# Attention followed by an ELU layer on one core: value matmuls ahead of the first step, an earlier weight block, and later slots for batch 2's transposes

## The chip, the cores and the metric

The kernel runs on one core of a Trainium2 chip. The metric is the device time of one execution in microseconds. Before: 322.39 us, the median of three executions (322.37 to 322.59). Each execution also reports its span (device time less some 1.7 us of start and end) and the mean clock granted to TensorE, where 1.0 is full speed. All executions in this study are of the state called fast; the last sections show that this name covers two groups with different clocks.

## The reference, cut to what matters

```python
scores = scale * q @ k.T + alibi_bias       # 8 batches, 8 heads, 576 positions, 64 per head
mask = (rel >= 0) & (rel < 128)             # each position sees itself and the 127 before it
attn = softmax(where(mask, scores, -1e9)) @ v
x = attn.transpose(0, 2, 1, 3).reshape(4608, 512)
h = x @ w_in                                # 512 -> 2048
out = where(h > 0, h, exp(min(h, 0)) - 1) @ w_out    # 2048 -> 512
```

## The kernel before

It is one hand-made schedule. Its slots are numbered, and a slot holds one group of hidden products (`x @ w_in`, L250), pieces of attention, and one group of output products (L269). Instructions reach each engine in the order in which they are emitted. A batch's q and k come in by DMA as `st`, and VectorE turns them to `QT` and `KT` (L139) for all batches from the third on (batch 2, counted from 0); the first two are turned by TensorE (L131). PSUM is the memory that TensorE writes its results to, in banks. The parts that matter here, with cuts marked:

```python
def turn_qk(b, w, h2, dh, ...):             # L139: VectorE transpose of a quarter of q or k
    V.transpose(o, st[b][...])              # needs all four loads of that q or k
def first_weigh(b, u, half):                # L183: the "product", exponentials times the bias table
    V.tensor_tensor(out=e, in0=e, in1=TAB[...], op=ALU.mult)
def values(b, i, part, bank=av):            # L215 on TensorE, then VectorE:
    ...                                     # L221 reciprocal, L222 normalization to xn
def turn(b, i, copy, bank):                 # L234 transpose of xn on TensorE, L235 copy to xT
    ...
def hidden(t, c0, w, f0, nf, p):            # L250, then L255 exponential on ScalarE,
    ...                                     # L256 clamp on GpSimd
def elu(...):                               # L263 on VectorE: g, which frees the PSUM bank p
    ...
# one slot: early tasks, hidden products, g of the slot before, tasks, output products, late tasks
```

"Freed product" below means the first L183 of batch 1 (slot 19): the values of slot 20 wait for it.

The softmax here doesn't subtract the row's maximum and nothing guards it: scores larger than these inputs give would overflow.

## Time and profile before

| What | Before |
|---|---|
| Median device time | 322.39 us |
| Span of the profiled execution | 320.7 us |
| TensorE busy | 312.4 us, 97% |
| TensorE's waits after the start | 3.1 us in all |
| Mean clock of the profiled execution | 1.00 |

TensorE's busy share leaves nothing to overlap: a wait that goes away shortens the kernel unless a later wait takes the gain back, and any other engine's busy time matters only where TensorE waits for it. So the list of TensorE's waits (who waits, for whom, us in all, how many, the longest) and the timelines around each one are the views to read. They are shown in the prediction. A line of a timeline has start, duration, engine, source line, operation, output and inputs, shape, count; a bracket gives the idle time before it and what ended it.

### The profile page before, as it was taken

How to read it: one execution, taken by the hardware profiler on the slowest of the kernel's cores; microseconds unless marked ns; L12 is line 12 of the kernel's file. 1: busy time of each engine (PE TensorE's matmuls, PEld its weight loads, DVE VectorE, ACT ScalarE, POOL GpSimd, SP SyncE). 2: the span in 40 equal slices, each digit the busy share in tenths (PEclk: the TensorE clock that was granted, in tenths of full speed). 3: DMA queues.
4: the chain of work that ended last, by engine and by line, in shares of the span. 5: the costliest groups of instructions: out<-in, count | busy, mean ns of one | idle time of the engine just before them, and what ended most of it. 6: DMA issues, size and time to landing. Idle time of an engine off the chain costs nothing.

```text
span 320.7 us, 9636 instructions
## 1 busy us (share of the span) xinstructions
PE 312.4 (97%) x4072; PEld 222.3 (69%) x4072; DVE 218.6 (68%) x446; ACT 183.9 (57%) x327; POOL 166.2 (52%) x254
## 2 busy tenths in 40 slices
PE   7999998999999999999999999999999999999996
PEld 7678873787777777777666666676677666766653
DVE  5457656888877877777877787778777566653330
ACT  6777456775655465556666666646654655543431
POOL 8467768284656546563756365655633333333320
PEclk9999999999999999999999999999999999999999
DMA  8999999977799939795979878994911111110012
GB/s 102 201 193 207 192 166 147 113 76 100 84 92 125 127 52 118 97 120 88 98 96 124 114 84 90 125 131 68 108 51 51 44 50 51 51 57 35 33 59 74
DMA packets 94043, 32.02 MB, mean 100 GB/s; under 512 B 81840, under 2 KB 89520, under 8 KB 94000
## 3 DMA queue, kind: packets, MB, share of 16 engines
q0 software_dynamic: 73600, 18.36, 62.6%
q1 hardware_dynamic: 20400, 13.05, 15.5%
q8 instruction: 32, 0.52, 0.7%
q14 instruction: 11, 0.09, 0.1%
HBM read 36.70 MB, written 9.44 MB: 144 GB/s over the span
## 4 chain that ended last, share of the span: by engine, by line
PE 91%; DVE 2%; POOL 2%; ACT 2%; DMA 1%; issue 0%; DVEq 0%; POOLq 0%; ACTq 0%
PE hp L250 38%; PE op L269 19%; PE av L269 16%; PE sp L215 4%; PE spa L192 4%; PE op L289 2%; POOL e L256 1%; DMA st<-in_k_dram 1%; PE sp L269 1%; PE spa L167 1%; PE av L283 1%; DVE xn L222 1%; ACT e L255 1%; DVE g L263 1%; PE sp L250 1%; POOL VP L109 1%
## 5 line engine op out<-in xcount | busy, mean ns | idle before, releaser
L256 POOL TENSOR_SCALAR e<-e 128x512 f32<-128x512 f32 x144 | 90.1, 626 | 141.2 <-ACT e L255 140.6
L250 PEld LDWEIGHTS <-wi 128*128 128x128 f16 x1856 | 124.5, 98 | 35.3 <-issue 5.2
L250 PE MATMUL hp<-xT,wi 128*128 128x128 f16 (+2 forms) x1760 | 146.0, 233 | 0.6 <-DVE g L263 0.6
L263 DVE SCALAR_TENSOR_TENSOR g<-e,hp 128x512 f16<-128x512 f32 x139 | 95.0, 683 | 56.1 <-POOL e L256 54.6
L255 ACT ACTIVATE e<-hp 128x512 f32<-128x512 f32 x139 | 83.3, 599 | 86.5 <-PE hp L250 83.4
L269 PE MATMUL op<-wo,g 128*128 128x512 f16 x304 | 77.5, 379 | 0.0
L269 PEld LDWEIGHTS <-g 128*128 128x128 f16 x560 | 50.1, 98 | 36.7 <-issue 1.1
L269 PE MATMUL av<-wo,g 128*128 128x512 f16 x240 | 61.4, 379 | 0.0
L203 DVE TENSOR_TENSOR EX<-EX,TAB 128x1024 f16<-128x1024 f16 x48 | 33.1, 690 | 15.4 <-ACT EX L198 15.3
L109 POOL DMA_DIRECT2D VP<-in_v_dram x40 | 35.0, 878 | 1.8 <-DMA wi<-in_moe_w_in_dram 1.3
L198 ACT ACTIVATE EX<-spa 128x512 f16<-128x512 f32 x48 | 26.1, 594 | 16.4 <-PE spa L192 16.4
L222 DVE TENSOR_TENSOR xn<-sp,rden 128x256 f16<-128x256 f32 (+1 forms) x60 | 25.4, 424 | 2.1
L198 ACT ACTIVATE EX<-sp 128x512 f16<-128x512 f32 x48 | 26.1, 600 | 0.0
L215 PEld LDWEIGHTS <-EX 128*128 128x128 f16 x576 | 22.3, 97 | 3.6 <-DVE EX L183 2.9
L215 PE MATMUL sp<-VP,EX 128*128 128x65 f16 x428 | 18.9, 193 | 1.3 <-DVE EX L183 1.3
L139 DVE STREAM_TRANSPOSE KT<-st 128x576 f16<-128x576 f16 x24 | 18.1, 801 | 2.0 <-DMA st<-in_k_dram 2.0
L139 DVE STREAM_TRANSPOSE QT<-st 128x576 f16<-128x576 f16 x24 | 18.3, 802 | 0.0
L276 ACT COPY ob<-op 128x512 f32<-128x512 f32 x19 | 11.1, 586 | 9.5 <-PE op L269 9.2
L103 POOL DMA_DIRECT2D st<-in_k_dram x24 | 16.5, 688 | 0.1
L103 POOL DMA_DIRECT2D st<-in_q_dram x24 | 16.3, 682 | 0.0
L192 PEld LDWEIGHTS <-KT 32*128 32x128 f16 x480 | 8.9, 93 | 10.4 <-issue 10.2
L192 PE MATMUL spa<-QT,KT 32*128 32x256 f16 (+2 forms) x240 | 14.7, 248 | 0.0
(88 smaller groups left out, 189.2 us busy)
## 6 DMA issues: line engine op xcount, KB each, us to landing
out_dram<-ob SPq DMA_DIRECT2D x35, 256.0 KB, 2.4
VP<-in_v_dram POOLq DMA_DIRECT2D x32, 128.0 KB, 4.4
st<-in_k_dram POOLq DMA_DIRECT2D x24, 144.0 KB, 3.5
st<-in_q_dram POOLq DMA_DIRECT2D x24, 144.0 KB, 4.0
wi<-in_moe_w_in_dram POOLq DMA_DIRECT2D x4, 512.0 KB, 12.0
wo<-in_moe_w_out_dram POOLq DMA_DIRECT2D x4, 512.0 KB, 11.7
s<-in_q_dram POOLq DMA_DIRECT2D x2, 384.0 KB, 9.3
VP<-in_v_dram POOLq DMA_DIRECT2D x8, 64.0 KB, 4.1
```

What stands on the lines that cost most here:

```text
L103: nc.gpsimd.dma_start(st[b][32 * g:32 * g + 32, w, :, :, :, :].rearrange("p h n j d -> p (h n) (j d)"), (q, k)[w][b, 2 * g:2 * g + 2, :, : ...
L109: nc.gpsimd.dma_start(VP[b % 2][0:p, n, :, 0:D], v[b, :, 128 * n:128 * n + p, :].rearrange("h p d -> p h d"))
L139: V.transpose(o, st[b][:, w, h2, n0:n1, :, 32 * dh:32 * dh + 32])
L192: nc.tensor.matmul(sp[g][:, 256 * h2 + o:256 * h2 + o + n], kt_[b % 2][r, k0:k0 + 128], QT[b % 2][r, h2, dh, q0:q0 + n], start=dh == 0, st ...
L198: nc.scalar.activation(unit(b, u)[:, g, :, :], sp[g].rearrange("p (h c) -> p h c", h=2), AF.Exp, scale=0.125)
L203: V.tensor_tensor(out=e, in0=e, in1=TAB[:, int(u == 3), 2 * gp:2 * gp + 2, :, :], op=ALU.mult)
L215: nc.tensor.matmul(a[:, x, h2, :], ex_[u][:, c:c + 128], VP[b % 2][:, n, 2 * g + h2, 0:D + 1], start=j == 0, stop=j == len(parts) - 1)
L250: nc.tensor.matmul(p[:, l * w + u0:l * w + u1], w_in_sb[:, c, fc * 128:(fc + 1) * 128], xT[:, c, x0:x0 + u1 - u0], start=(c == 0), stop=(c ...
L255: nc.scalar.activation(e[:, 0:n], p[:, 0:n], AF.Exp)
L256: nc.gpsimd.tensor_scalar(out=e[:, 0:n], in0=e[:, 0:n], scalar1=1.0, scalar2=0.0, op0=ALU.min, op1=ALU.max)
L263: V.scalar_tensor_tensor(out=gs[t][:, f0:f0 + nf, c0:c0 + w], in0=sh(es.pop((t, c0, f0))), scalar=1.0, in1=sh(hps.pop((t, c0, f0))), op0=A ...
L269: nc.tensor.matmul(o, gs[t][:, fc, ts * 128:(ts + 1) * 128], w_out_sb[:, fc, :], start=(fc == 0), stop=(fc == NFC - 1))
```

## The change

Its intent: let the first half of the second tile's values run before the first hidden step, so that their normalization is done earlier; bring the third quarter of `w_in` sooner; and keep batch 2's transposes out of the way of the product, with their loads sooner.

```diff
         load_first(0, 0, 1)
+        load_wi(2)
         load_v(0, 2)
-        load_wi(2)
         load_wi(3)
@@
         for half in range(2):
             first_expo(0, 1, half, half, 0, 128)
+        values(0, 1, 0)
@@
-        at(0, values, 0, 1, 0)
         at(0, values, 0, 1, 1, op)
@@
-        for n, s in enumerate((6, 7, 11, 12, 14)):
+        for n, s in enumerate((6, 7, 11, 12, 13)):
             at(s, load_v, 1, n)
@@
-        TURN = 18, 18, 22, 23, 24, 25, 26, 28
+        TURN = 19, 22, 23, 24, 24, 25, 27, 29
@@
-                at(a - 8 + n if a else 15 + (n + 1) // 2, load_qk, b, int(n < 4), n % 4)
+                at(a - 8 + n if a else 14 + n // 2, load_qk, b, int(n < 4), n % 4)
             for n in range(5):
-                at(a + 3 + n if a else 19 + n, load_v, b, n)
+                at(a + 3 + n if a else 18 + n // 2, load_v, b, n)
```

I call the three parts part 1 (values), part 2 (`w_in`) and part 3 (slots and loads of batch 2).

## The prediction

> **What bounds the kernel now.** I read the head of the page first, then who TensorE waited for, then the timeline around each wait that is left.
>
> ```profile
> PE 312.4 (97%) x4072; PEld 222.3 (69%) x4072; DVE 218.6 (68%) x446; ACT 183.9 (57%) x327; POOL 166.2 (52%) x254
> ...
> PEclk9999999999999999999999999999999999999999
> ```
>
> TensorE is busy for 312.4 of 320.7 us, with the full clock granted in every slice. From 76 us to the final output matmuls it has no gap, so a change before 76 us is worth just what it takes off the moment at which that stretch begins. The change removes no work. Its ceiling is thus TensorE's waits before 76 us, which the table of TensorE's waits lists in full:
>
> ```profile
> PE op L289 <- DVE ident L312: 1.6, 1, 1.6
> PE sp L215 <- DVE EX L183: 1.3, 1, 1.3
> PE op L234 <- DVE xn L222: 1.0, 1, 1.0
> PE hp L250 <- DVE g L263: 0.6, 2, 0.3
> PE spa L161 <- ACT EX L172: 0.2, 1, 0.2
> ```
>
> The columns are us in all, how often, and the longest. The first, 1.6 us, is the start of the kernel and isn't touched. The rest is 3.1 us, or 1.0% of 322.39: no outcome near 2% faster is in reach. The change aims at the second line (batch 2's transposes) and the third (the second tile's values). How the second arises shows in the timelines of TensorE and VectorE:
>
> ```profile
> 50.65 1.04 PE L269 MATMUL sp<-wo,g 128*128 128x512 f16 x4
> 53.02 0.30 PE L215 MATMUL sp<-VP,EX 128*128 128x65 f16 x4 [1.34 <-DVE EX L183]
> ...
> 48.66 1.02 ACT L172 ACTIVATE EX<-spa 128x1024 f16<-128x1024 f32 x1 [0.94 <-PE spa L167]
> ...
> 50.93 1.49 DVE L139 STREAM_TRANSPOSE KT<-st 128x576 f16<-128x576 f16 x2 [2.00 <-DMA st<-in_k_dram]
> 52.32 0.65 DVE L183 TENSOR_TENSOR EX<-EX,TAB 128x1024 f16<-128x1024 f16 x1
> ```
>
> The exponentials that the product (L183) weighs are ready at 48.66 + 1.02 = 49.68 us. VectorE starts it at 52.32, since two transposes of batch 2 stand before it in its queue and wait for the fourth load of k, issued at 47.67 and landed 3.1 us later. TensorE's values wait for the product.
>
> The third wait:
>
> ```profile
> 14.24 1.07 PE L250 MATMUL hp<-xT,wi 128*128 128x128 f16 x16
> 15.14 0.41 PE L215 MATMUL av<-VP,EX 128*128 128x65 f16 x8
> 15.39 0.40 PE L215 MATMUL op<-VP,EX 128*128 128x65 f16 x8
> 16.83 0.38 PE L234 MATMUL op<-ident,xn 128*128 128x128 f16 x4 [1.04 <-DVE xn L222]
> 17.05 1.95 PE L250 MATMUL hp<-xT,wi 128*128 128x128 f16 x32
> ...
> 16.03 0.61 POOL L256 TENSOR_SCALAR e<-e 128x512 f32<-128x512 f32 x1 [3.30 <-ACT e L255]
> 16.70 0.68 DVE L263 SCALAR_TENSOR_TENSOR g<-e,hp 128x512 f16<-128x512 f32 x1
> 17.29 0.42 DVE L235 COPY xT<-op 128x512 f16<-128x512 f16 x1
> ```
>
> The second tile's transpose (L234) waits for the two normalizations that follow the two halves of its values.
>
> **What the Trainium skill says.** "TensorE: Matmul & The Clock Gate", in the table that opens it (engine queue depth): VectorE's queue is strictly first in, first out. The trace agrees: a product ready at 49.68 starts at 52.32. The same page, Part 2, back-to-back issue gap: N/2.4 + 2.5 ns, so 216 ns at N = 512. The L269 groups agree (58.31 to the next group at 59.17: 4 in 0.86 us). So the values at 53.02 could have issued at 50.65 + 0.88 = 51.53, and the stall is worth 1.49 us, more than the 1.34 shown, which counts from a modelled end. "GPSIMD Engine Reference", section 1: GpSimd shares its SBUF interface with VectorE. The trace agrees: L256 takes 0.61 us mostly, but 1.00 at 70.56, where a product runs on VectorE.
>
> **Part 1, half of the second tile's values ahead of the first step.** TensorE now does 8 value matmuls at 14.24 (0.25 us), then 16 of the first step from 14.49, then the other 8 from 15.39 as before. The operands are there: the half's exponentials end at 13.86, its v landed at 9.3. The first half's reciprocal and normalization move from 15.59 to about 14.7, out of the way. The second half's start when its matmuls end, 15.82; 0.18 + 0.42 us and hand-overs give 16.44 instead of 16.77. The transpose issues at 16.50 instead of 16.83: 0.33 gained. But the first step's matmuls end 0.25 later, and so do its exponential (15.59 to 16.19), GpSimd's clamp (16.28 to 16.89) and VectorE's g (from 16.95 instead of 16.70). The order of VectorE's instructions is unchanged here, and g stands ahead of the copy of the transposed tile to xT. The copy starts 0.59 after g, at 17.54, and ends at 17.96. The second 16 of the 32 matmuls at 17.05 need that copy. Before they issued at 17.05 + 0.89 = 17.94; now TensorE is ready at 17.62 and held to about 18.01. Part 1: 0.07 us lost, in effect nothing.
>
> **Part 2, w_in's third quarter ahead of v.** From the issues and their times to landing: that quarter landed at 8.28 + 13.1 = 21.4 us and its first use is the step at 23.32, without a wait. It will land near 20.5; the v block it passes lands near 21.4, against a use at 25.56. The first copies' order in the queue is otherwise unchanged. Worth 0.
>
> **Part 3, batch 2.** Its loads go out one to three slots sooner, the fourth k load at about 44.0 instead of 47.67. The data in flight before it (the last v of batch 1, three k loads) landed by 49.35; 144 KB more at the some 180 GB/s of this stretch is 0.8 us, so it lands between 48 and 50.2. VectorE does the product at 49.73 to 50.40, and one transpose from 50.33 to 51.15. The values issue at 51.53 instead of 53.02: 1.49 gained. VectorE is free again before their reciprocal is due at 51.87, so the next product runs 52.43 to 53.11 and the next values at 53.16 instead of 54.66: the gain holds. From there to 60.9 TensorE and VectorE alternate by the same chain as before, all 1.49 earlier.
>
> What comes back: the displaced transpose lands in slot 24 (slots are the kernel's own schedule steps), where VectorE had little room. In times of the before trace: transposes at 61.29 and 62.03, g at 62.75 (was 62.00), product at 63.33 (was 62.58), another transpose at 63.92, and then g of slot 25 from 64.66 to 65.35 (was 64.31 to 65.00). The hidden product of slot 27, at 65.14, reuses that g's PSUM bank: it starts at 65.40, 0.26 lost. The later moves (27 and 29 for 26 and 28) fall behind products that TensorE then waits less for. The wait of 0.26 at 72.33 stays: it follows matmul, exponential, a clamp of 1.0 and g. GpSimd issues two loads between clamps in slots 14 to 17; 2 x 0.67 + 0.61 = 1.95 us against a slot of 1.75 delays the clamps of 15 and 16 by 0.1 to 0.2 us, which their buffers, a ring of three, take up.
>
> **Sum.** 322.39 + 0.07 - 0 - 1.49 + 0.26 = 321.23 us.
>
> **Rivals.** (A) Part 1 pays in full: were the copy not behind g, 0.33 would be kept, and the time 320.8. For it: the 1.04 us wait is real. Against: the copy's place in VectorE's queue. (B) The k loads land late, because they now share the DMA queues with v of batch 1, as its loads took 5.7 to 12.5 us. If the fourth came after 51.1, the one transpose would hold the reciprocal behind it. At 52 us, about 0.9 of the 1.49 would be lost: 322.1. Against: the k loads took 3.1 to 5.3 us. (C) The room in slots 24 to 28 is larger than I work out (GpSimd's clamps shorten when the products move), so nothing is given back: 321.0. (D) More transposes collide than counted, VectorE being 90% busy from 58 to 66 us, and waits at 63.58 and 66.04 come too, 0.3 each: 321.8.
>
> **Range and chances.** The sum moves by +0.3 for each step of VectorE's queue misjudged, by -0.4 for A, by +0.9 for B; repeats differ by 0.2. I predict 321.2, with 320.5 to 322.0 to hold it 8 times in 10. Faster than 315.9 would need twice the waits that exist: 0.005. Slower than 328.8 would need a load 6 us late: 0.01. Within 2%: 0.985.
>
> **What would show it.** Step by step in the changed profile: the wait of 1.3 on L183 is gone, the first batch 1 product starts within 0.1 of its exponential's end, and one transpose follows it without a wait on a DMA. The 1.0 wait of L234 shrinks to some 0.7 and a new one of about 0.3 appears in the first hidden matmuls, on the copy L235. A wait of L250 on g L263 of about 0.2 appears some 14 us after the removed one. From the start of batch 2's first scores on, everything is alike, 1.1 to 1.2 earlier than at 76.40. I am wrong if those scores start later than 75.9, or if a wait on batch 2's loads stands in the chain.

## The result, and the profile after

The changed kernel took 320.69 us (median of 6 executions, 320.55 to 321.19); the kernel before took 322.57 in the same rounds (6 executions, 322.37 to 324.06). Their ratio is 0.9932, with a 95% interval of 0.991 to 0.9954. A ratio is the mean time of one kernel's fast runs over the mean of the other's in the same rounds, so it is not quite the ratio of the medians. (For kernels with few runs the recorded ratio isn't that of all the runs of the kernel before that the record lists. It evidently takes a part of them, and which part isn't on record. So the means by clock below are the safer figures.) Applied to 322.39 the ratio gives 320.2 us, a gain of 2.2 us, where I had forecast 1.2 and a low end of 320.5. The medians differ by 1.9, the spans of the two profiled executions by 1.7 (320.7 and 319.0).

The head of the page and the list of TensorE's waits, changed kernel:

```profile
PE 312.1 (98%) x4072; PEld 222.0 (70%) x4072; DVE 219.0 (69%) x446; ACT 183.9 (58%) x327; POOL 165.4 (52%) x254
...
PEclk9999999999999999999999999999999999999999
```
```profile
PE op L289 <- DVE ident L312: 1.6, 1, 1.6
PE op L234 <- DVE xn L222: 0.7, 1, 0.7
PE hp L250 <- DVE g L263: 0.5, 2, 0.3
PE spa L161 <- ACT EX L172: 0.2, 1, 0.2
PE hp L250 <- DVE xT L235: 0.2, 1, 0.2
```

The work is the same. The wait for the product is gone, the one for the normalization is 0.3 shorter, and a new one on the copy L235 stands in the list. The timelines around the freed product (TensorE's two lines, then VectorE's):

```profile
50.52 1.04 PE L269 MATMUL sp<-wo,g 128*128 128x512 f16 x4
51.40 0.29 PE L215 MATMUL sp<-VP,EX 128*128 128x65 f16 x4
...
49.60 0.69 DVE L183 TENSOR_TENSOR EX<-EX,TAB 128x1024 f16<-128x1024 f16 x1 [0.79 <-ACT EX L172]
50.61 0.82 DVE L139 STREAM_TRANSPOSE KT<-st 128x576 f16<-128x576 f16 x1 [0.32 <-DMA st<-in_k_dram]
```

The product now starts at 49.60, as soon as its exponentials are there, and the values follow the output products without a wait: 0.88 us from group to group. The transpose still waits 0.32 us for its load, but behind the product, where nothing needs VectorE until the reciprocal at 51.72. The early timeline, TensorE and then VectorE:

```profile
14.22 0.42 PE L215 MATMUL av<-VP,EX 128*128 128x65 f16 x8
16.50 0.38 PE L234 MATMUL op<-ident,xn 128*128 128x128 f16 x4 [0.73 <-DVE xn L222]
17.98 1.07 PE L250 MATMUL hp<-xT,wi 128*128 128x128 f16 x16 [0.20 <-DVE xT L235]
...
16.90 0.69 DVE L263 SCALAR_TENSOR_TENSOR g<-e,hp 128x512 f16<-128x512 f32 x1 [0.45 <-POOL e L256]
17.50 0.42 DVE L235 COPY xT<-op 128x512 f16<-128x512 f16 x1
```

The transpose L234 came 0.33 us sooner, and the third group of hidden products then waited for the copy behind g. It started at 17.98; the prediction's working put it at 17.94 before and about 18.01 after. Slot 27, VectorE's g of slot 25 and the hidden product that reuses its bank:

```profile
62.94 0.64 DVE L263 SCALAR_TENSOR_TENSOR g<-e,hp 128x512 f16<-128x512 f32 x1
...
63.63 1.05 PE L250 MATMUL hp<-xT,wi 128*128 128x128 f16 x16
```

How far TensorE is ahead of the kernel before, read off its starts in the two profiles:

| Point on TensorE | Before | After | Ahead |
|---|---|---|---|
| TensorE's turn of the first batch's rest (L131) | 18.93 | 18.98 | -0.05 |
| Scores of slot 3 (L161) | 21.60 | 21.49 | 0.11 |
| Values of slot 20 | 53.02 | 51.40 | 1.62 |
| Hidden products of slot 26 | 63.58 | 61.95 | 1.63 |
| Hidden products of slot 27 | 65.14 | 63.63 | 1.51 |
| Hidden products of slot 31 | 72.33 | 70.71 | 1.62 |
| First scores of batch 2 | 76.40 | 74.78 | 1.62 |
| Last matmul group | 316.45 | 314.82 | 1.63 |

So these two executions differ by 1.6 us, and nearly all of it is the one wait. That still isn't the 2.2 us of the ratio. The times of the kernel before gave the hint: four of its six executions took 322.4 to 322.6, but two took 323.75 and 324.06.

### The profile page after: what moved, and what is told of

The parts are those of the page before. It is cut to its first block, busy times and chain, and to the rows that moved or that the text cites. A ratio compares the mean times of both kernels' runs of the same rounds, so it can differ in the third digit from the quotient of the medians.

```text
span 319.0 us, 9636 instructions
## 1 busy us (share of the span) xinstructions
PE 312.1 (98%) x4072; PEld 222.0 (70%) x4072; DVE 219.0 (69%) x446; ACT 183.9 (58%) x327; POOL 165.4 (52%) x254
## 4 chain that ended last, share of the span: by engine, by line
PE 89%; DVE 4%; POOL 2%; DMA 2%; ACT 2%; issue 1%; DVEq 0%; POOLq 0%; ACTq 0%
PE hp L250 37%; PE op L269 20%; PE av L269 16%; PE spa L192 4%; PE sp L215 4%; DMA s<-in_q_dram 2%; DVE g L263 1%; PE sp L269 1%; POOL e L256 1%; PE av L131 1%; PE av L283 1%; ACT e L255 1%; DVE QT L139 1%; PE spa L167 1%; PE sp L250 1%
## 5 line engine op out<-in xcount | busy, mean ns | idle before, releaser
L192 PE MATMUL sp<-QT,KT 32*128 32x256 f16 (+2 forms) x240 | 14.7, 248 | 0.0
```

The costliest lines, as they stand in the source:

```text
L192: nc.tensor.matmul(sp[g][:, 256 * h2 + o:256 * h2 + o + n], kt_[b % 2][r, k0:k0 + 128], QT[b % 2][r, h2, dh, q0:q0 + n], start=dh == 0, st ...
```

## The experiments

Theory at the start: the whole gain is the product freed from the transposes; parts 1 and 2 are worth nothing; the rest is scatter. Rivals: parts 1 and 2 carry some of it; the sooner loads are needed; a slow group of executions has something to do with it, and then the question is what. All kernels gave the right result. The experiments' times are five rounds each, in three calls on three chips. "Full" means a mean clock of 0.998 or more, "low" below 0.996 (mostly 0.995); no run lies between. Two sets of runs of the same kernel in one call have full-clock means of 322.21 and 322.49, so a difference of 0.3 us between such means is no finding. In the profiles TensorE's first hidden products start anywhere from 13.80 to 14.24 us in the kernels that leave the work before them alone, so lengths between two points of a profile are safer than its times.

| Kernel | Full: runs, mean us | Low: runs, mean us |
|---|---|---|
| Before, all of its runs beside the experiments, and its repeat | 82, 322.32 | 38, 323.85 |
| Its repeat alone | 13, 322.49 | 9, 323.71 |
| Part 1 alone | 8, 322.61 | 6, 323.78 |
| Part 2 alone | 13, 322.37 | 9, 323.85 |
| Part 3 alone | 6, 320.83 | 0 |
| Slots alone | 6, 320.82 | 0 |
| Loads alone | 19, 321.88 | 3, 323.86 |
| Gap filled | 14, 322.47 | 0 |
| Late load | 0 | 4, 326.19 |
| Changed kernel, first rounds | 6, 320.76 | 0 |
| Changed kernel again | 6, 320.80 | 0 |
| Spread turns | 7, 320.73 | 0 |
| Copy first | 6, 320.77 | 0 |
| Both mends combined | 6, 320.39 | 0 |

### Control: the kernel before again

No edit.

> The kernel before, unchanged, as a control. All theories: ratio 1.000 within 0.003. It tells whether the 0.16 us by which the fourth group of 16 hidden matmuls was stretched in the first profile (20.54 to 21.60 us, 1.06 instead of 0.90) belongs to the kernel or to that one execution. Theory 'scatter': the group takes 0.90 this time in its place, and the span is 0.1 to 0.2 us shorter. Rival 'the early w_in block cured it': it is stretched again.

Ratio 1.0 (0.9984 to 1.0016). The stretched group took 0.94 us (20.40 to 21.34) this time, and the span was 320.6. Of the 22 executions 9 had a clock of 0.995 and took 323.2 to 324.4. So the kernel before has two groups of executions, 1.5 us apart (323.85 against 322.32 over all of its runs), and the share of the upper one differs between calls: 21 of 51, 5 of 28 and 3 of 19 beside the experiments, on chips 4, 8 and 3. Whether that goes with the chip is not shown.

### Part 1 alone

```diff
             first_expo(0, 1, half, half, 0, 128)
+        values(0, 1, 0)
...
-        at(0, values, 0, 1, 0)
```

> Only the half of the second tile's values goes ahead of the first step. Theory 'the copy of the transposed tile stands behind g': TensorE's wait on L234 falls from 1.04 to 0.73, a new wait of 0.2 on the copy L235 appears, the turn of the first-tile rows (L131 at 18.93) starts within 0.1 us of before, ratio 0.999 to 1.001. Rival 'part 1 pays in full': L131 starts 0.3 earlier and the time falls by 0.3 us, ratio 0.999.

Ratio 0.9998 (0.9974 to 1.0022). L234's wait fell to 0.73, a wait of 0.21 on L235 appeared, and L131 started at 18.88. From the scores before it (L167, 13.79) that is 5.09 us, against 18.93 - 13.91 = 5.02 in the kernel before: 0.07 lost, as worked out. At full clock the mean is 322.61, no better than the kernel before (322.21 and 322.49). Part 1 is worth nothing, by the mechanism that I gave.

### Part 2 alone

```diff
         load_first(0, 0, 1)
+        load_wi(2)
         load_v(0, 2)
-        load_wi(2)
```

> Only w_in's third quarter goes ahead of v. Theory 'no one waits for it': no wait of TensorE changes, ratio 1.000 within 0.001. Rival 'it cures the stretched group at 20.54': that group takes 0.90 and the time falls by 0.16 us.

Ratio 1.0004 (0.9987 to 1.002). The stretched group took 0.90 us (20.23 to 21.13), which the rival had asked for. But in other kernels with part 2 in them it took 1.35 (spread turns) and 1.49 (copy first), and without part 2 0.94 (the control): it is scatter, not part 2.

The profile of this kernel happened to catch an execution of the upper group. The stretches of one us from 52 to 57 (columns: stretch and length, then busy us and count of TensorE, its weight loads, VectorE, ScalarE and GpSimd, then the granted clock, the DMA share and GB/s), and one timeline line of TensorE:

```profile
52.00:53.00 1.00, 0.01 (x1) 0.01 (x1) 0.93 (x2) 0.00 (x0) 1.00 (x2) 0.80 1.18 202
53.00:54.00 1.00, 1.00 (x9) 0.49 (x10) 0.54 (x3) 0.00 (x0) 1.00 (x3) 0.50 1.55 216
54.00:55.00 1.00, 1.00 (x3) 0.30 (x2) 0.67 (x2) 0.97 (x1) 0.73 (x2) 0.50 1.94 174
55.00:56.00 1.00, 1.00 (x8) 0.51 (x8) 0.00 (x0) 0.06 (x1) 0.00 (x0) 0.50 2.41 156
56.00:57.00 1.00, 1.00 (x8) 0.42 (x9) 0.95 (x3) 0.57 (x2) 0.00 (x0) 0.99 2.42 154
...
53.87 1.89 PE L269 MATMUL sp<-wo,g 128*128 128x512 f16 x4
```

TensorE is idle from 51.2 to 53.0, waiting for the product. In that time its clock falls to half, and it stays there: (1 - 0.80) / 0.5 = 0.40 us in the first stretch, then 3, then 0.02, together 3.42 us, from 52.60 to 56.02. The fall comes 1.4 us into the wait; from 49 us to its start TensorE was busy throughout. The output group that takes 1.04 us at full clock takes 1.89. Half of 3.42 is 1.71 us of lost clock, or 0.995 as a mean over the span of 321.7: the figure that marks the whole upper group. Since 0.39 us of the 3.42 still lie in the wait, which ends at 52.99, the work itself loses (3.42 - 0.39) / 2 = 1.5 us, which is the distance between the two groups.

### Part 3 alone

```diff
-        TURN = 18, 18, 22, 23, 24, 25, 26, 28
+        TURN = 19, 22, 23, 24, 24, 25, 27, 29
...
-        for n, s in enumerate((6, 7, 11, 12, 14)):
+        for n, s in enumerate((6, 7, 11, 12, 13)):
-                at(... 15 + (n + 1) // 2, load_qk, ...)
+                at(... 14 + n // 2, load_qk, ...)
-                at(... 19 + n, load_v, b, n)
+                at(... 18 + n // 2, load_v, b, n)
```

> Only batch 2's slots and loads move. Theory 'the whole gain is the product freed from the transposes': the first values of batch 1 issue 1.5 us earlier (about 51.5 instead of 53.02), batch 2's first scores 1.5 to 1.6 earlier (74.8 to 74.9), time 1.5 to 1.7 us less, ratio 0.995. Rival 'parts 1 and 2 carry some of the 1.9 us': 1.2 us or less, ratio 0.9963 or above.

Ratio 0.9928 (0.9901 to 0.9955). The values of slot 20 issued at 51.47, batch 2's first scores at 74.86. At full clock the gain over the kernel before is 322.21 - 320.83 = 1.4 us in these rounds; the expected 1.5 to 1.7 is met within the scatter of 0.2. The ratio says 2.3, because runs of the upper group count in it: they were 21 of the 51 of the kernel before here, and over all 51 the means differ by 2.1. Part 3 carries all of the change.

### Slots alone

```diff
-        TURN = 18, 18, 22, 23, 24, 25, 26, 28
+        TURN = 19, 22, 23, 24, 24, 25, 27, 29
```

> Only the slots of batch 2's transposes move; all loads stay where they were, so the fourth k load lands at about 50.8 as before. Theory 'the order in VectorE's queue is the whole of it': the product starts at 49.7, the one transpose at about 50.9 and ends at 51.7, just before the reciprocal is due at 51.9; the values issue at 51.5, batch 2's first scores at 74.8 to 74.9, time 1.5 to 1.7 less. Rival 'the sooner loads are needed too': the transpose holds the reciprocal back, and the gain is under 1.2.

Ratio 0.9939 (0.9915 to 0.9963). The values issued at 51.26 and batch 2's first scores at 74.63. The mean of 320.82 is that of part 3 alone. VectorE's timeline:

```profile
49.46 0.69 DVE L183 TENSOR_TENSOR EX<-EX,TAB 128x1024 f16<-128x1024 f16 x1 [0.79 <-ACT EX L172]
50.50 0.83 DVE L139 STREAM_TRANSPOSE KT<-st 128x576 f16<-128x576 f16 x1 [0.35 <-DMA st<-in_k_dram]
```

With the load in its old place the transpose starts at 50.50, no later than in the changed kernel. The order in VectorE's queue is the whole of it; the sooner loads add nothing that the times show.

### Loads alone

```diff
-                at(... 15 + (n + 1) // 2, load_qk, ...)
+                at(... 14 + n // 2, load_qk, ...)
```

with the two loads of v as in part 3.

> Only the loads go sooner; two transposes stay ahead of the product. In the trace of the changed kernel the fourth k load, issued 3.6 us sooner, landed at 50.5, just 0.3 before the 50.8 of the kernel before. Theory 'the queues are full, sooner issues buy little': the transposes start at about 50.6, the values at 52.7, 0.3 us gained. Rival 'the late load was the cause': the load lands by 49 and at least 1.0 us is gained.

Ratio 0.9988 (0.9973 to 1.0002). The transposes started at 50.52 instead of 50.93, but TensorE too is ahead in this profile, by 0.53 us:

```profile
50.12 1.04 PE L269 MATMUL sp<-wo,g 128*128 128x512 f16 x4
52.62 0.40 PE L215 MATMUL sp<-VP,EX 128*128 128x65 f16 x4 [1.47 <-DVE EX L183]
```

By the starts the wait is 52.62 - 50.12 - 0.88 = 1.62 us, no shorter than the 1.49 of the kernel before. The fourth k load, issued over 3 us sooner, took 6.2 us instead of 3.1, probably because it queues behind loads that are already in flight. The full-clock mean is 322.29 - 321.88 = 0.4 below that of the kernel before in these rounds; as the same kernel's sets differ by 0.3, and this profile does not show a shorter wait, it stays open where that comes from. Three of 22 runs are still in the upper group. The profile caught one of them, and its half clock lasts 3.42 us as well, from 52.30 to 55.72.

### Gap filled

The kernel before, with idle matmuls in the wait:

```diff
+        at(20, warm, 20)
         for u, a0, a1, d in ((0, 18, 19, 2), ...
```

> The kernel before with 20 idle matmuls of 128 columns (20 x 0.056 = 1.1 us) put into the 1.5 us in which TensorE waits for the freed product; the wait itself stays, so the work after it starts when it did. Theory 'TensorE's idle stretch lets its clock fall to half for some 3 us in part of the executions': no execution has a mean clock of 0.995 or less, none is above 323.2 us, the median is that of the full-clock executions of the kernel before, 322.2 to 322.5, and the mean is 0.4 to 0.7 us below that of the kernel before. Rival 'the slow executions have another cause': about a third of them are still at 323.3 to 324.5 with a mean clock of 0.995.

Ratio 0.9995 (0.9982 to 1.0008); in these rounds just 3 of 19 runs of the kernel before were in the upper group, so a mean 0.4 lower wasn't to be had: 322.47 against 322.64, 0.2 less. The clock is what decides it: none of 14 executions was low, the slowest took 323.10. TensorE:

```profile
51.53 1.28 PE L289 MATMUL op<-ident 128*128 128x128 f16 x20
53.11 0.30 PE L215 MATMUL sp<-VP,EX 128*128 128x65 f16 x4 [0.30 <-DVE EX L183]
```

The values are as late as before, 53.11, but the array was busy until shortly before. A wait filled with useless work costs 1.5 us and no clock. At a share of 38 in 120 the chance of 0 in 14 is (82/120)^14 = 0.005; at the 3 of 19 of these rounds it would be (16/19)^14 = 0.09, so this run alone is not proof. The next one settles it.

### Late load

The kernel before, with the fourth k load behind the first q load, so that TensorE waits longer:

```diff
-                at(a - 8 + n if a else 15 + (n + 1) // 2, load_qk, b, int(n < 4), n % 4)
+                (at if a or n != 3 else before)(a - 8 + n if a else 18 if n == 3 else 15 + (n + 1) // 2, load_qk, b,
+                                                int(n < 4), n % 4)
```

(A first form of this edit read a tile before its load was issued, was found at fault before it ran, and was mended.)

> The kernel before with the fourth k load issued behind the first q load, some 0.7 us later: TensorE's wait grows from 1.5 to about 2.2 us. Both theories: full-clock executions 0.6 to 0.8 us slower, 323.0. Theory 'the idle stretch halves the clock, the more often the longer it is': two thirds or more of the executions have a mean clock of 0.995 or less (a third of the kernel before's). Rival 'not tied to the wait': a third, as before.

Ratio 1.012 (1.0104 to 1.0136). The wait grew far more than I expected:

```profile
55.02 0.40 PE L215 MATMUL sp<-VP,EX 128*128 128x65 f16 x4 [3.87 <-DVE EX L183]
```

All four executions were low (three at 0.989, one at 0.995), so there is no full-clock time to compare, and the expected 0.6 to 0.8 us can't be checked. In the profile the half clock lasts from 53.1 to 59.9 us, 6.84 us by the sum used above, or twice 3.42, and the mean clock is 0.989. The clock falls some 1.95 us into the wait. Two of the slowest runs of the kernel before, 325.33 and 325.42, show 0.988 as well. The share of low executions rises with the wait: 0 of 14 with the array kept busy, 38 of 120 at about 1.5 us (and 18 of 58 in the kernels of part 1, part 2 and the loads alone, which keep that wait), 4 of 4 at 3.9. The length of the wait alone doesn't decide it: by the lists of waits 1.61 us in the control left the clock full, and 1.47 with the loads alone did not.

### The changed kernel again

No edit.

> The changed kernel once more. Theory: no execution at a clock of 0.995, all between 320.3 and 321.6; against the full-clock executions of the kernel before 1.5 to 1.6 us less, against all of them 1.9 to 2.1 less (ratio 0.9935 to 0.994). Rival 'the 1.9 us are all from the wait': the full-clock executions of before are 1.9 us or more above it.

Ratio 0.9953 (0.9941 to 0.9965), mean clock 0.998 or more in all six. At full clock 322.42 - 320.80 = 1.6 us in the same rounds, as expected. The ratio is nearer to 1 than expected: it corresponds to 322.32 for the kernel before, so it took few low runs or none. Over all 19 runs of the kernel before, 3 of them low, the means differ by 1.8. In this profile the wait on L235 doesn't appear; the second group of hidden products waits 0.28 us for its block of `w_in` instead, and slot 3 has a hold of 0.29 (see copy first).

### Spread turns

```diff
-        TURN = 19, 22, 23, 24, 24, 25, 27, 29
+        TURN = 19, 22, 23, 26, 24, 25, 27, 29
```

> The changed kernel with the displaced fourth k transpose in slot 26, where none is, instead of slot 24, where it stands with another. Theory 'two transposes in one slot delay g, and with it the hidden product of slot 27': that product, 0.12 late in the changed kernel, is no longer late, but the later wait on g in slot 31 grows by the same 0.1, so batch 2's first scores move by less than 0.05. Rival 'the loss stays': they start 0.1 us earlier.

Ratio 0.9935 (0.9911 to 0.9958). From the values of slot 20 to batch 2's first scores TensorE took 74.80 - 51.53 = 23.27 us, against 74.78 - 51.40 = 23.38 in the changed kernel. The hidden product of slot 27 isn't late any more, and the wait in slot 31 did not grow. My theory here fell: the 0.11 stays gained in the trace. It is too little to see in the times.

### Copy first

```diff
-BUF[s % 2 if s < 4 else (s + 1) % 3 if s < 18 else (s + 1) % 2]
+BUF[s % 3 if s < 18 else (s + 1) % 2]
...
-        before(1, done, 0)
         before(1, turn, 0, 1, V.tensor_copy)
+        before(1, done, 0)
```

> The changed kernel with the copy of the second tile to xT ahead of the first g on VectorE, and the hidden products of slots 0 to 17 in a plain ring of three banks (so that the third one does not need that g). Theory 'g ahead of the copy took part 1's gain': the wait of 0.2 on L235 goes, the copy starts at 16.9, L131 starts at 18.6 instead of 18.98, 0.35 us less than the changed kernel if no later wait takes it. Rival 'another wait takes its place' (v, w_in or the ring): less than 0.1.

Ratio 0.9938 (0.9913 to 0.9962), mean 320.77: no gain that the times show. In the trace the copy starts at 16.58, the wait on L235 is gone, and from the first hidden products to L131 TensorE takes 18.25 - 14.13 = 4.12 us instead of 18.98 - 14.47 = 4.51. So g did take part 1's gain. But shortly after it is lost:

```profile
19.86 0.34 PE L250 MATMUL hp<-xT,wi 128*128 128x128 f16 x3
20.63 0.89 PE L250 MATMUL hp<-xT,wi 128*128 128x128 f16 x13 [0.42 <-issue]
```

The group of slot 3 is held after its third matmul. Part 1 alone, spread turns, the gap filled and the changed kernel again show the same hold there, of 0.34, 0.28, 0.45 and 0.29 us. In most other profiles the group is just stretched, in two (0.90 us) it is not. "Issue" means that the profile knows no releaser. Each profile has a packet of the instruction queue between 17 and 19 us, so TensorE may wait there for its own instructions; no run shows that, and it stays open.

### Both mends combined

The changed kernel with the last two edits together.

> The changed kernel with both mends: the copy to xT ahead of the first g with a plain ring of three banks, and the fourth k transpose in slot 26. Theory 'each mend is taken by another wait' (the fourth group of hidden matmuls held at its fourth matmul; VectorE's g of slot 29): within 0.2 us of the changed kernel in the same rounds. Rival 'they add up': 0.4 us less or more.

Ratio 0.994 (0.9928 to 0.9952), median 320.40 (320.11 to 320.67), mean 320.39, against 320.80 for the changed kernel in the same rounds. The times side with the rival: 0.41 us less. But the two ranges overlap by 0.3 us on six runs each, and sets of the same kernel differ by 0.3, so it is a likely gain and not a sure one. In the trace the hold in slot 3 was short this time (20.02 to 21.05 for the group, 1.03 us), and batch 2's first scores issue at 74.39 instead of 74.78; of these 0.39 us, 0.19 are there already at the first values (14.03 against 14.22), before either mend. It has the lowest mean here.

## Why the prediction was right or wrong

**What bounds the kernel: half right, and the failing step.** I wrote that TensorE has "the full clock granted in every slice", and from it that the ceiling of the change was "TensorE's waits before 76 us", 3.1 us. Both hold for the execution whose profile I read. But 38 of 120 executions of the same kernel have a mean clock of 0.995 or less, which is what 3.42 us at half clock give, and take 323.85 instead of 322.32. The profiles that caught such executions place the half clock in the wait that the change removes and just after it. In the prediction's terms "the stall is worth 1.49 us" was the mis-sized term: on the average execution it is worth those 1.5 us and 38/120 x (323.85 - 322.32) = 0.48 us more. The changed kernel's own median, 320.69, lies in my range; the gain on the kernel before does not. None of my rivals had it, and my range allowed for less. The filled gap, the late load and 43 of 43 full-clock executions without the wait show the cause.

Added up: at full clock the changed kernel's 12 runs average 320.78, which is 322.32 - 320.78 = 1.54 below the kernel before; with the 0.48 it is 2.0 us. The first ratio gives 2.2 and the second 1.5; they differ with the low executions among the runs of the kernel before that each takes.

**Part 1: right.** The copy waited behind g as worked out, the new wait was 0.20, and L131 started 0.05 later. Alone it measures 0.9998. Rival A is excluded as the kernel stands, though copy first shows that its reason was sound.

**Part 2: right.** Nothing waited for that block.

**Part 3: the gain right, the reason for the loads wrong.** The values issued at 51.40; from the scores of slot 3 to the values of slot 20 the gain is 1.62 - 0.11 = 1.51, worked out as 1.49. But the sooner loads did not matter. The fourth k load landed at about 50.5, later than my 48 to 50.2, and "one transpose follows it without a wait on a DMA" was wrong: it waited 0.32. VectorE had room to wait, though not much: in the profile of both mends combined the load came 0.91 late, and the transpose ran to 51.59, past the reciprocal's start at 51.49. Rival B was that near.

**What comes back: mis-sized.** I gave 0.26 lost in slot 27 for good; it was 1.63 - 1.51 = 0.12, too short to stand in the list of waits, where I had looked for it, g ending at 63.58 where my working, taken 1.63 earlier, has 63.72. And I wrote that "the wait of 0.26 at 72.33 stays": it became 0.15, so the loss was paid back. GpSimd's clamp before that g took 0.80 us instead of 1.0. That is rival C's reason and, by 76 us, its outcome, though it came after the slots that C named. Rival D did not come about.

**The sum.** At full clock 1.16 was forecast and 1.54 measured: 0.26 from the loss that did not last, and 0.12 that lies within the 0.2 by which repeats differ. The other 0.5 is the clock.

## What to carry to other kernels

A wait of the matmul engine can cost more than its length: if it lets the clock fall, the work after it runs slow too, and only in some executions, so one profile at full clock does not show it. Look at the clock of every execution, and split the runs by it, before a gain is worked out or a ratio believed. Where an engine takes its queue strictly in order, first ask what stands in front of the instruction that others wait for; moving it ahead of two transposes did here what loads issued 3 us sooner could not.

## What the Trainium skill lacked or had wrong

- "TensorE: Matmul & The Clock Gate", Part 1, says that the clock falls to half after an idle window of about 3.4 us which runs freely, and the table in "Why this matters for your kernels" warns of gaps over about 3 us. The windows of the half clock agree (3.42 us with part 2 alone, 6.84 with the late load), and so does the variation from run to run. The length of the gap doesn't: a wait of some 1.5 us sufficed in 38 of 120 executions, and in the two profiles that caught a fall in such a wait (the loads alone and part 2 alone) it came 1.1 and 1.4 us into it.
- The same page does not say how the chance of a fall depends on the length of a single short gap. The runs give three points: 0 of 14 with the gap filled to 0.3 us, 38 of 120 at about 1.5 us, 4 of 4 at 3.9 us.
- The same page advises against idle gaps; it does not say that idle matmuls can bridge a wait in mid-kernel. 20 of them did, with no low execution in 14, though the 0.2 us that they saved in their rounds lies within the interval (0.9982 to 1.0008).
- "DMA: Bandwidth & Descriptors", "Anatomy of one DMA", fits about 2.0 us plus bytes over 436 GB/s, an estimate of 2.3 us for the 144 KB of a k load. The four k loads of batch 2 took 3.1 to 5.3 us in the kernel before and, issued sooner, 6.3 to 6.8 in the changed one. The fit has no term for loads already in flight; that these are the cause is likely, but was not tested.
- No page names the hold of TensorE in slot 3, 0.28 to 0.45 us in five profiles with no releaser.
